# Moving one batch's query transposes behind sixteen score matmuls, and one re-lay one unit later, in an attention and gated feed-forward kernel

## The chip, the core and the metric

The kernel runs on one core of a Trainium2 chip. The core has five engines with a queue of instructions each: TensorE (PE in the profile; its weight loads are listed apart as PEld), VectorE (DVE), ScalarE (ACT), GpSimd (POOL) and SyncE (SP). They run side by side and wait for each other through semaphores. Matmul results land in a small accumulator memory, PSUM, of eight banks; everything else lives in SBUF. Transfers are carried out by 16 DMA engines. The metric is the device time of one execution in microseconds, as the median of several runs; less is better.

## The reference

Two stages follow one another. The first is attention with a sigmoid in the place of the softmax, for 8 batches, 12 heads, 448 positions and a head width of 64:

```python
scores = scale * np.matmul(q, k.transpose(0, 1, 3, 2)) - np.log(S)
attn = 1.0 / (1.0 + np.exp(-scores))
return np.matmul(attn, v).astype(np.float32)
```

Its output, seen as x with 8 · 448 = 3584 rows of 12 · 64 = 768 columns, goes through a gated feed-forward layer of width 1536:

```python
gate = np.maximum(x @ w_gate, 0.0)
val = x @ w_val
return (gate * val @ w_out).astype(np.float32)
```

Inputs and outputs are 32-bit floats; the kernel multiplies in 16 bits.

## The kernel before

**Tiling.** Heads are taken in three groups g of four. The 448 positions of a batch are seven chunks c of 64. Queries and keys have to lie transposed (head width on the partitions) before the scores can be formed; the transposed form of one group is a tile `qkT` with 14 blocks, seven for the keys and seven for the queries. The scores of one key chunk against all queries are a score unit: matmuls of 64x64 tiles at L259, four of them running side by side in the four quarters of TensorE's array, then a sigmoid on ACT (L187) into a tile `PT`. Seven such units give what the product with the values needs (`pv`, L277, again 64x64 tiles). DVE scales its result out of PSUM into `xT` (L184), which is the input of the feed-forward layer. A feed-forward unit (`gv`, L342) forms one 128-column block of gate and value: six full-array 128x128 matmuls `g_ps`, six `v_ps`, then a relu on ACT (L354) or DVE (L356) and a product on DVE (L363) into `hT`. From batch 1's end on, feed-forward products are formed with fewer multiplications from sums and differences of blocks (Strassen's scheme, L409, L738); DVE forms those sums at L400 and L597, and `T` from the weight `wo`.

**Order.** Nothing reorders instructions: `tc.manual_schedule()` leaves each engine's order as the program writes it, and waits are set from the data. PSUM banks go round in a ring: four banks in the first stage, eight later.

**Batch 0**, the first 29 us, has its own order. The queries are split in two halves, of 4 and 3 chunks (`QCUT` = 4), so that there are six slots: slots 0 to 2 are the groups with the first half of the queries, slots 3 to 5 the groups with the second. A slot has four score units `slot.unit(u)`: the first three hold two key chunks (8 matmuls each in slots 3 to 5, of 64x192), the last one chunk (4 matmuls). The scores of a unit go to one of two two-bank PSUM buffers (`pairp`, `bufs=2`), which alternate. So a unit cannot start before the sigmoid of the unit two before it has read that buffer. What TensorE does between the units is written in a table `after`, keyed by slot and unit; each entry runs right behind the unit named. In the parts that matter here it holds the `pv` of an earlier slot, `second_queries()` (the PE transposes, L204, of the second half of the queries of groups 1 and 2: 3 chunks x 2 heads x 2 groups = 12 matmuls against the identity, each 64 columns of the array wide, and two DVE copies L211 into `qkT`), and `ffn_mix(1)`, which takes one feed-forward unit off a queue (its first use takes a unit of 256 columns of batch 0).

**Batch 1** runs bursts of score units, each followed by `ffn_mix` with a number of feed-forward units (`mix`). Its `hooks` name what happens between the units of a burst: an entry `(n, job)` runs when n units of the mix are left. `steps` are DVE instructions that form weight sums, handed out between the units by the counts in `given`. When n units are left, the hooks come first, then the steps, then the unit.

**Re-lays.** From batch 2 on the transposes are left to the DMA: `dma_transposes(b, g)` has DVE copy the four heads' keys and queries (L242, two copies) into a tile `rel` (two buffers), and SP issues one transposing DMA from `rel` into `qkT` (L246). The last burst of batch 1 (burst 5, a mix of four units) has two hooks: `late_loads` with four units left, and the re-lay of batch 2's group 2 with two left.

**Loads.** POOL's queue issues the loads, converting to 16 bits, in program order. `late_loads` first makes POOL wait for the transposing DMA of batch 2's group 1 (`hold`, L887, a tiny copy), then loads v of batch 2 (L115, L117), k and q of batch 3 (L111; these overwrite batch 2's k and q and so wait for the copies L242 of the re-lay), and the weight `wo` in two parts (L164).

**Around the end.** Each `y` unit of the output projection goes to the result by SP's queue (L382), from 104 us on.

Of the kernel before, what the change touches and what calls it, by code (L numbers as in the profile page):

```python
# [18 lines left out]
def kernel(  # L19
# [170 lines left out]
    def qkT_of(b, g):  # L190
        if (b, g) not in qkT_tiles:
            qkT_tiles[(b, g)] = qkTp.tile([P, TW, P], FP16, tag="qkT", name="qkT")
        return qkT_tiles[(b, g)]

    def pe_transposes(b, g, ti, c0=0, c1=NCH):
        transposed(b, g, ti, c0, c1)()
# [21 lines left out]
    def quarter_transposes(b, g):  # L218
        qkT = qkT_of(b, g)
        trt = [bank16("trt") for _ in range(2)]  # L220
        for i in [*range(NCH, TW), *range(NCH)]:
            t16 = in_tiles[b][i // NCH]
            c = i % NCH
            for h in range(2):
                for r in range(2):
                    rows = slice(64 * r, 64 * r + 64)
                    nc.tensor.transpose(  # L227
                        trt[r][64 * h : 64 * h + 64, 64 * i : 64 * i + 64],
                        t16[rows, 2 * g + h, c * D : (c + 1) * D],
                        ident[rows, rows],  # L230
                    )
        for r in range(2):
            nc.vector.tensor_copy(
                qkT[:, :, 64 * r : 64 * r + 64],
                trt[r][:, 0 : TW * 64].rearrange("p (i x) -> p i x", i=TW),
            )

    def dma_transposes(b, g):
        k16, q16, _ = in_tiles[b]
        rel = relp.tile([P, TW, P], FP16, tag="rel", name="rel")  # L240
        for ti, t16 in enumerate((k16, q16)):
            nc.vector.tensor_copy(  # L242
                rel[:, ti * NCH : (ti + 1) * NCH, :].rearrange("p c (h d) -> p h c d", h=2),
                t16[:, 2 * g : 2 * g + 2, :].rearrange("p h (c d) -> p h c d", c=NCH),
            )
        nc.sync.dma_start_transpose(  # L246
            qkT_of(b, g)[:], rel[:].rearrange("p c x -> p (c x)")
        )
# [331 lines left out]
    def early_sum_steps(j, f):  # L580
        views = []
        for i in range(3 * j, 3 * j + 3):
            t = early.tile([P, 2, 512], FP16, tag=f"PT{i}", name="S")
            flat = t[:].rearrange("p a y -> p (a y)")[:, 0 : HD * 2 * P]
            views.append(flat.rearrange("p (x y) -> p x y", y=2 * P))
        yield lambda: gate_sums(f, f + 2)
        yield from unit_sum_steps(("s", f), f, views)
# [206 lines left out]
    def ffn_mix(count, hooks=(), steps=(), given=()):  # L794
        hooks = list(hooks)
        for left in range(count, -1, -1):
            while hooks and hooks[0][0] >= left:
                hooks.pop(0)[1]()
            for step in itertools.islice(steps, given[count - left] if steps else 0):
                step()  # L800
            if left:
                gv_queue.popleft()()
# [16 lines left out]
    slots = [FirstSlot(half * NG + g, g, half) for half in range(2) for g in range(NG)]  # L819
    push_first(0, range(0, 2), False)  # L820
    gv_queue.append(lambda: gv_two(0, 0, 64 * HALVES[0][1], 2))
    def second_queries():
        for g in range(1, NG):
            pe_transposes(0, g, 1, QCUT, NCH)
# [8 lines left out]
        keys(0, 3)  # L833
        keys(3, NCH)

    def pv_then_queries():
        slots[2].pv()
        second_queries()

    def two_pv():  # L840
        slots[3].pv()
        slots[4].pv()
# [12 lines left out]
        (2, 1): lambda: pe_transposes(0, 0, 1, QCUT, NCH),  # L855
        (2, 2): slots[0].pv,
        (2, 3): slots[1].pv,
        (3, 0): pv_then_queries,
        (3, 2): lambda: ffn_mix(1),
        (4, 0): lambda: ffn_mix(1),  # L860
        (4, 2): lambda: ffn_mix(1),
        (5, 0): two_pv,
# [86 lines left out]
    for b in range(1, B):  # L949
# [12 lines left out]
        if b == 1:  # L962
            mix = (4, 3, 3, 3, 3, 4)
            hooks = {
                1: [(3, lambda: quarter_transposes(1, 1))],
                4: [(2, lambda: dma_transposes(2, 0)), (0, lambda: dma_transposes(2, 1))],
                5: [(4, late_loads), (2, lambda: dma_transposes(2, 2))],
            }
            steps = itertools.chain.from_iterable(early_sum_steps(j, 2 * j) for j in range(4))
            given = ((0, 0, 1, 0, 2), (0, 1, 1, 1), (0, 1, 1, 1), (0, 1, 1, 0), (2, 0, 0, 0), (0, 1, 1, 1, 0))  # L970
        else:
            mix = (0,) * count
# [111 lines left out]
```

## Time and profile before

| | |
|---|---|
| median of 3 runs | 387.45 us (387.33 to 387.62) |
| profiled execution | 387.08 us |
| its span | 385.3 us |
| busy: PE / PEld | 379.8 us (99%) / 223.0 us |
| busy: DVE / ACT / POOL | 304.7 us (79%) / 227.2 us (59%) / 51.2 us (13%) |
| chain that ended last | PE 97%, ACT 2% |
| granted TensorE clock | 0.999 of full speed |
| DMA | 43.81 MB, mean 114 GB/s |

The span is the time from the first to the last recorded instruction; the profiled execution's own time, 387.08 us, is the span and 1.8 us around it. A row of the timeline has the start in us, the time for which the row's instructions run, the engine, the line, the operation, the tile written and the tile read, the shapes, the number of instructions merged into the row, and in brackets the idle time ahead of it and what ended it. Since matmuls are pipelined, the time from one row's start to the next row's start on PE is what a block costs, not the busy time beside it. A row of the windows has, for each stretch, its length, the busy time and the number of instructions of PE, PEld, DVE, ACT and POOL, the granted clock, the DMA share and the GB/s.

### The profile page before, as it was taken

Reading aid. Unit: us, or ns where it says so; the run is one execution under the profiler, and the core shown is the slowest. Engines: PE = TensorE matmul, PEld = TensorE weight load, DVE = VectorE, ACT = ScalarE, POOL = GpSimd, SP = SyncE. Lnnn points to the kernel's source line nnn. Section 1 sums busy time; section 2 is a strip of 40 time slices with the busy share of each in tenths; the row PEclk is TensorE's granted clock in tenths of the full one; section 3 lists DMA queues with packets and bytes.
Section 4 is the critical chain, followed back from the end, with each engine's and each line's share of the span. In section 5 each row is a group of like instructions: output and inputs, shape, how many; then the busy total and the mean of one; then the engine's idle time right before and its main releaser. Section 6 shows DMA issues by size and latency. Waiting matters only on the chain.

```text
span 385.3 us, 9098 instructions
## 1 busy us (share of the span) xinstructions
PE 379.8 (99%) x3626; PEld 223.0 (58%) x3626; DVE 304.7 (79%) x611; ACT 227.2 (59%) x480; POOL 51.2 (13%) x77
## 2 busy tenths in 40 slices
PE   8999999999999999999999999999999999999996
PEld 6678876885555545555555554545555555555664
DVE  3455668769868999999868789999978788999663
ACT  5967887558777645555777764545577344333322
POOL 9643305003300003000302300000000000000000
PEclk9999999999999999999999999999999999999999
DMA  9999999996998303952499994222012220000335
GB/s 174 198 199 204 204 200 142 207 204 109 169 209 196 83 0 43 171 100 49 70 242 146 204 213 80 48 49 48 2 40 71 72 68 2 0 2 0 77 89 164
DMA packets 67595, 43.81 MB, mean 114 GB/s; under 512 B 35680, under 2 KB 64224, under 8 KB 67552
## 3 DMA queue, kind: packets, MB, share of 16 engines
q0 software_dynamic: 28992, 23.24, 41.0%
q1 hardware_dynamic: 37792, 19.34, 25.0%
q10 hardware_dynamic: 768, 0.66, 0.6%
q8 instruction: 28, 0.46, 0.5%
q14 instruction: 15, 0.12, 0.1%
HBM read 47.19 MB, written 11.01 MB: 151 GB/s over the span
## 4 chain that ended last, share of the span: by engine, by line
PE 97%; ACT 2%; DVE 0%; issue 0%; ACTq 0%
PE u L409 35%; PE g L409 16%; PE y L409 12%; PE qk_ps L259 10%; PE pv_ps L277 8%; PE g_ps L342 5%; PE v_ps L342 5%; PE u L738 2%; PE g L738 2%; ACT PT L187 2%; PE warm_ps L175 1%; PE trt L204 1%; PE trt L227 0%; DVE qkT L211 0%; DVE ysb L564 0%
## 5 line engine op out<-in xcount | busy, mean ns | idle before, releaser
L187 ACT ACTIVATE PT<-qk_ps 128x448 f16<-128x448 f32 (+3 forms) x318 | 151.1, 584 | 79.2 <-PE qk_ps L259 79.0
L409 PEld LDWEIGHTS <-S 128*128 128x128 f16 x576 | 56.4, 98 | 45.9
L648 DVE TENSOR_TENSOR gsb<-g,gsb 128x448 f32<-128x448 f32 x72 | 42.7, 624 | 7.8 <-PE g L409 7.5
L259 PE MATMUL qk_ps<-qkT 64*64 64x448 f16 (+2 forms) x756 | 47.3, 336 | 0.6 <-ACT PT L187 0.3
L409 PEld LDWEIGHTS <-hT 128*128 128x128 f16 x318 | 29.5, 98 | 24.0 <-issue 6.1
L277 PE MATMUL pv_ps<-PT,v 64*64 64x448 f16 (+2 forms) x756 | 36.4, 329 | 0.2 <-ACT PT L187 0.2
L488 DVE SCALAR_TENSOR_TENSOR ysb<-y,ysb 128x384 f32<-128x384 f32 x33 | 18.4, 556 | 20.7 <-PE y L409 14.1
L184 DVE TENSOR_SCALAR xT<-pv_ps 128x448 f16<-128x448 f32 (+2 forms) x53 | 27.8, 566 | 7.1 <-PE pv_ps L277 5.9
L409 PEld LDWEIGHTS <-wg 128*128 128x128 f16 x216 | 20.1, 98 | 21.8 <-issue 4.3
L409 PEld LDWEIGHTS <-wv 128*128 128x128 f16 x216 | 21.1, 98 | 19.7
L470 ACT ACTIVATE ysb<-u 128x384 f32<-128x384 f32 x28 | 13.8, 491 | 30.9 <-PE u L409 26.8
L409 PE MATMUL u<-wo,hT 128*128 128x384 f16 x156 | 29.8, 327 | 0.0
L259 PEld LDWEIGHTS <-qkT 64*64 64x64 f16 x756 | 17.7, 105 | 20.4 <-issue 14.3
L277 PEld LDWEIGHTS <-v 64*64 64x64 f16 x756 | 21.4, 107 | 11.1 <-issue 0.6
L111 POOL DMA_DIRECT2D k<-in_k_dram x15 | 11.5, 770 | 93.8 <-DVE rel L242 88.1
L409 PE MATMUL u<-xT,wg 128*128 128x448 f16 x108 | 23.5, 354 | 0.0
L409 PE MATMUL g<-xT,wg 128*128 128x448 f16 x108 | 23.4, 352 | 0.0
L409 PE MATMUL u<-X,wv 128*128 128x448 f16 x108 | 23.4, 352 | 0.0
L409 PE MATMUL g<-xT,S 128*128 128x448 f16 x108 | 23.4, 352 | 0.0
L409 PE MATMUL g<-X,S 128*128 128x448 f16 x108 | 23.4, 352 | 0.0
L409 PE MATMUL u<-X,S 128*128 128x448 f16 x108 | 23.4, 352 | 0.0
L409 PE MATMUL u<-xT,wv 128*128 128x448 f16 x108 | 23.4, 352 | 0.0
(103 smaller groups left out, 563.7 us busy)
## 6 DMA issues: line engine op xcount, KB each, us to landing
out_dram<-ysb SPq DMA_DIRECT2D x53, 192.0 KB, 3.6
v<-in_v_dram POOLq DMA_DIRECT2D x8, 336.0 KB, 11.0
v<-in_v_dram POOLq DMA_DIRECT2D x16, 168.0 KB, 10.3
wo<-in_moe_w_out_dram POOLq DMA_DIRECT2D x2, 1152.0 KB, 19.8
k<-in_k_dram POOLq DMA_DIRECT2D x10, 224.0 KB, 11.8
k<-in_k_dram POOLq DMA_DIRECT2D x3, 672.0 KB, 12.0
q<-in_q_dram POOLq DMA_DIRECT2D x3, 672.0 KB, 14.6
q<-in_q_dram POOLq DMA_DIRECT2D x8, 224.0 KB, 12.2
```

What stands on the lines that cost most here:

```text
L111: nc.gpsimd.dma_start(t16[:, xs, cs], rows_of(src, b)[:, xs, cs])
L175: nc.tensor.matmul(ps[:, 0:n], zeros[:, 0:P], zeros[:, 0:n], start=True, stop=True)
L184: nc.vector.tensor_scalar(out=xT, in0=src, scalar1=XSCALE, scalar2=None, op0=AOP.mult)
L187: nc.scalar.activation(PT_ap, ps_ap, AF.Sigmoid, bias=sig_bias, scale=qk_scale)
L259: nc.tensor.matmul(out_of(hh)[o : o + 64, :], qkT[rows, c, cols], qkT[rows, NCH + c0 : NCH + c1, cols], start=True, stop=True, tile_positi ...
L277: nc.tensor.matmul(ps[hh][64 * r : 64 * r + 64, 0:qn], v16[rows, 2 * g + hh, c * D : (c + 1) * D], pieces[c][rows, hh, :], start=(c == 0), ...
L342: nc.tensor.matmul(ps[:, 0:qn], (wg, wv)[i][:, dc, f * P : (f + 1) * P], xT_tiles[b][:, dc, q0 : q0 + qn], start=(dc == 0), stop=(dc == ND ...
L409: nc.tensor.matmul(ps[:, 0:n], A[:, k_, :], W[:, k_, :], start=(first and k_ == 0), stop=(k_ == kn - 1), skip_group_check=True,)
L470: nc.scalar.activation(o, ps[:, 0:HM], AF.Copy, scale=OUT_SCALE)
L488: nc.vector.scalar_tensor_tensor(out=o, in0=ps[:, 0:HM], scalar=OUT_SCALE, in1=o, op0=AOP.mult, op1=AOP.add)
L648: nc.vector.tensor_tensor(out=gs[u][i][:], in0=ps[u][:, 0:S], in1=gs[u][i][:], op=AOP.add)
L738: nc.tensor.matmul(ps[j // 2][:, j % 2 * SQ : (j % 2 + 1) * SQ], sets[j][i][:, k_, :], W[:, k_, :], start=(first and j % 2 == 0 and k_ == ...
```

## The change

There are two edits. In batch 0's table, the twelve query transposes of `second_queries()` stood behind the `pv` of slot 2, after unit (3, 0). Now the `pv` of slot 2 stands there alone, units (3, 1) and (3, 2) follow it directly (sixteen score matmuls), and the transposes come behind unit (3, 2), in front of the feed-forward unit that was there already. In batch 1's last burst, the re-lay of batch 2's group 2 runs when one unit of the mix is left, not two. So on DVE its two copies change places with one weight sum (L597) and the product `hT` of the third feed-forward unit. The order on ACT, POOL and SP stays as it was; no instruction is added or taken away.

```diff
-    def pv_then_queries():
-        slots[2].pv()
+    def queries_then_unit():
         second_queries()
+        ffn_mix(1)
...
-        (3, 0): pv_then_queries,
-        (3, 2): lambda: ffn_mix(1),
+        (3, 0): slots[2].pv,
+        (3, 2): queries_then_unit,
...
-                5: [(4, late_loads), (2, lambda: dma_transposes(2, 2))],
+                5: [(4, late_loads), (1, lambda: dma_transposes(2, 2))],
```

## The prediction

> **What bounds the kernel now.** I read the page first, then TensorE's timeline around 17 us (the first edit) with ACT's rows beside it, then DVE, SP and POOL around 60 us (the second edit), and last the later readers of what those move.
>
> ```profile
> PE 379.8 (99%) x3626; PEld 223.0 (58%) x3626; DVE 304.7 (79%) x611; ACT 227.2 (59%) x480; POOL 51.2 (13%) x77
> PE 97%; ACT 2%; DVE 0%; issue 0%; ACTq 0%
> ```
>
> PE is busy 99% of the span and carries 97% of the chain, so an edit counts by what it does to PE's starts. Here is PE's timeline at the first edit, start to start:
>
> ```profile
> 15.62 0.96 PE L277 MATMUL pv_ps<-PT,v 64*64 64x256 f16 x28
> 16.38 0.36 PE L259 MATMUL qk_ps<-qkT 64*64 64x192 f16 x8
> 16.55 0.96 PE L277 MATMUL pv_ps<-PT,v 64*64 64x256 f16 x28
> 17.44 0.53 PE L204 MATMUL trt<-ident,q 128*64 128x128 f16 x12
> 17.89 0.52 PE L259 MATMUL qk_ps<-qkT 64*64 64x192 f16 x16
> 18.35 0.83 PE L342 MATMUL g_ps<-xT,wg 128*128 128x256 f16 x6
> ...
> 19.77 0.52 PE L259 MATMUL qk_ps<-qkT 64*64 64x192 f16 x12
> 20.22 0.83 PE L342 MATMUL g_ps<-xT,wg 128*128 128x256 f16 x6
> ```
>
> The same 28-matmul value product costs 0.76 us when scores follow (15.62 to 16.38) and 0.89 us when transposes follow (16.55 to 17.44). The scores are of the same 64*64 form as the product, the transposes are 128*64: a change of form costs about 0.13 us. Now ACT around it, each row from a narrow window:
>
> ```profile
> 16.86 0.81 ACT L187 ACTIVATE PT<-qk_ps 128x768 f16<-128x768 f32 x1
> 18.36 1.51 ACT L187 ACTIVATE PT<-qk_ps 128x768 f16<-128x768 f32 x2 [0.70 <-PE qk_ps L259]
> ```
>
> The first row is the sigmoid of unit (3, 0), which ends at 17.67; the second holds those of (3, 1) and (3, 2). ACT idles 0.70 us between them since the scores of (3, 1) come late. DVE at the second edit:
>
> ```profile
> 58.66 0.41 DVE L363 TENSOR_TENSOR hT<-gate_sb,v_ps 128x256 f16<-128x256 f32 x1
> 58.99 0.39 DVE L242 COPY rel<-k 128x896 f16<-128x896 f16 x1
> 59.29 0.39 DVE L242 COPY rel<-q 128x896 f16<-128x896 f16 x1
> 59.59 0.55 DVE L597 TENSOR_TENSOR S<-S,wg 128x768 f16<-128x768 f16 x1
> 60.06 0.35 DVE L363 TENSOR_TENSOR hT<-gate_sb,v_ps 128x192 f16<-128x192 f32 x1
> ...
> 60.80 0.35 DVE L363 TENSOR_TENSOR hT<-gate_sb,v_ps 128x192 f16<-128x192 f32 x1
> 62.36 0.62 DVE L184 TENSOR_SCALAR xT<-pv_ps 128x448 f16<-128x448 f32 x1 [1.22 <-PE pv_ps L277]
> ```
>
> DVE then has 1.22 us to spare. PE and the DMA later on:
>
> ```profile
> 60.00:65.00 5.00, 5.00 (x63) 2.56 (x60) 3.71 (x10) 4.37 (x10) 3.90 (x7) 1.00 0.79 126
> 80.00:85.00 5.00, 5.00 (x55) 5.00 (x54) 3.94 (x9) 3.37 (x8) 0.00 (x0) 1.00 1.16 211
> 105.00:110.00 5.00, 5.00 (x62) 2.84 (x59) 4.26 (x9) 4.45 (x10) 0.00 (x0) 1.00 1.40 143
> ```
>
> PE is busy throughout; the last column shows loads at 211 GB/s alone and 143 GB/s where a transposing DMA runs among them.
>
> **The first edit, step by step.** The new order on PE is value product, (3, 1), (3, 2), transposes, feed-forward unit.
> 1. Value product with scores behind it: 0.76, so (3, 1) starts at 16.55 + 0.76 = 17.31, not 17.89.
> 2. Eight scores take 0.17 (16.38 to 16.55), so PE reaches (3, 2) at 17.48. But its PSUM buffer is that of (3, 0), whose sigmoid ends at 17.67. PE resumes 0.05 after a sigmoid: at 28.85 a value product goes on, released by ACT, and the three sigmoids ahead of it end at 26.69 + 2.11 = 28.80. So (3, 2) starts at 17.72: a new wait of 0.24. Before, 17.67 had passed when PE got there. Behind it on PE stand the transposes and the feed-forward unit.
> 3. Sixteen scores with a change of form behind them take 0.46 (17.89 to 18.35). Less 0.19 for the first eight (0.17 and 0.02 for the slower start of that block after a change of form) this leaves 0.27 to 0.29, and the transposes start at 18.00.
> 4. The twelve transposes took 0.45 with scores behind them. With a 128*128 matmul behind them no warm row shows the price. Below: eight transposes followed by eight more take 0.25 (8.14 to 8.39) and followed by scores 0.32 (8.39 to 8.71), so without a change of form 0.45 less 0.07 to 0.09, about 0.36. Above: at 5.25 eight took 0.54 ahead of a 128*128 matmul, but the eight ahead of those took 0.42 against 0.25 at 8.14, so 0.17 of it is a slower array; 0.37 remains, 0.05 over 0.32, hence 0.50. I take 0.45, because the form changes here too. The unit starts at 18.45, bounds 18.36 to 18.50, against 18.35: +0.10 (+0.01 to +0.15).
> 5. A wait goes. Unit (4, 0) shares a buffer with (3, 2), whose sigmoid ended at 18.36 + 1.51 = 19.87, while PE was there at about 19.85. Twelve scores took 0.45 (19.77 to 20.22); sixteen with no such wait take 0.46 (17.89 to 18.35), four cost 0.08, so twelve should take 0.38. The sigmoids of (3, 1) and (3, 2) now come about 0.6 and 0.2 us sooner, hence -0.07.
>
> Sum: +0.03 us, bounds -0.06 to +0.08. The Trainium skill's page TensorEngine Tiling (Array Packing), section Key Properties, says that changing the tiling mode drains TensorE; by it three changes become two and the edit gains about one drain, -0.13 by the rows above. The rows agree that a change costs that; the rule leaves out the wait of step 2.
>
> Off the path: the two copies L211 (0.61) shift from 18.21 to about 18.4, end near 19.05, before DVE's next instruction at 19.22, and their reader (4, 0) comes at 19.85. `xT`, ready at 18.30, is in time for the unit. ACT keeps its order and waits for scores later too (0.28 at 20.15), so its lead is not passed on. No DMA, SP or POOL instruction moves here.
>
> **The second edit.** The third `hT` comes after its `v_ps` (58.85 + 0.66 = 59.51), at about 59.6 and not 60.06; the copies run at about 59.9 to 60.6, not 58.99 to 59.68; the last `hT` at about 60.98, not 60.80. Its bank is next written by the `g_ps` at 62.64, and DVE's 1.22 us of slack takes up the 0.18. A gain from the earlier third `hT` is excluded: PE waits for no bank here. SP issues the transposing DMA about 0.9 late (59.75 to 60.65); SP's next entry is at 81.78, so nothing queues behind it. POOL issues the load of k that waits for the copies at 63.28, 2.7 us after their new end; its hold waits for another group's DMA and opens at 60.80 as before. The DMA landed in 4.0 us, now 64.7. Its buffer `rel` is next written by DVE at 81.64, and its scores come after 87.7. If it took 17.4 us, as the one issued at 95.28 did among loads, it would land at 78.1, still in time. What it takes from the loads: `wo`'s second part landed at 65.8 + 22.1 = 87.9 and is first read at 93.15 (5.2 us to spare); q of batch 3 landed at 64.13 + 11.8 = 75.9 and is read at 81.33 (5.4). Full traffic of the transposing DMA is some 2 us, so at most 2 us of it moves into the loads. Cost 0 as long as the delay is under 5.2 us.
>
> Total +0.03 us: 387.08 becomes 387.11 in the profiled execution, which lies 0.37 under the median of the runs, so the median goes from 387.45 to 387.48, say 387.5. 0.2%, or 0.77 us, is about what a measurement of this kernel can tell from no change.
>
> **Rivals.**
> - The drain is saved and nothing takes its place: if (3, 2) is not held, step 2's 0.24 goes and the sum is -0.21: 387.25. For it speaks the 0.13 of the change of form; against it the buffers that alternate and the sigmoid's end at 17.67. It needs a sigmoid that ends before 17.43. This would still be no measurable change.
> - ACT's lead of 0.6 us is carried on to the end of batch 0. The PE waits on ACT that the views show are 0.3 us in the list of waits and 0.16 at 28.85, so with the rival above at most -0.7: 386.8; 0.2% is passed only if more such waits are hidden in blocks that the views show as busy. Against it: ACT waits for PE's scores, 79.0 us in the list, not the reverse.
> - Slower, by the loads. The transposing DMA no longer ends before the loads begin to move (about 63.6) and runs among them. At 143 against 211 GB/s over a landing of 17.4 us, the loads lose 17.4 x 0.32 = 5.6 us; `wo` would then come 0.4 late: 387.9. Held back over all 23 us of loads they lose 23 x (211/143 - 1) = 11 us, 5.8 beyond the margin: 393. It decides from 5.2 us of delay. Against it: at 95.28 the transposing DMA was issued 2 us behind the first loads, here it is issued 0.6 us ahead of them (61.28). The Trainium skill's page DMA: Bandwidth & Descriptors, section Queues, rings and completion order, says that a DMA engine takes turns between its queues packet by packet, which speaks for this rival. The rows above agree at 105 to 110 us, not at 80 to 85, though a transposing DMA was issued at 81.78.
>
> **How the numbers follow.** Forecast as summed (387.5): 0.58. Drain saved (387.25): 0.21. ACT's lead to the end: 0.06, of which 0.03 passes 0.2%. Loads: 0.07, of which 0.06 passes 0.2%. Something that no row shows: 0.08, of which 0.03 faster and 0.05 slower by over 0.2%. Faster by over 0.2%: 0.06; within: 0.83; slower: 0.11. The range 386.9 to 388.0 takes in the bounds of the first edit (387.2 to 387.55), the spread of the runs (0.17 up, 0.12 down) and the mild ends of the second and third rival.
>
> **What would show it.** Right: (3, 1) at 17.31, a stop of about 0.24 ahead of (3, 2) ended by ACT, transposes at 18.00, `g_ps` at 18.4 to 18.5, twelve scores in 0.38, and every later PE row shifted by under 0.1. The copies L242 at 59.9, the transposing DMA at 60.65, `wo` landed before 93. Wrong: `g_ps` before 18.25; a PE wait on DVE at L342 near 62.6; `T` from `wo` later than 93.2, or `rel` later than 81.7.

## The result, and the profile after

The changed kernel's median is 387.49 us (386.57 to 395.56, 22 executions), that of the kernel before, run beside it, 387.12 us (386.70 to 387.78, 22 executions). The ratio is 1.0023 with a 95% interval of 1.0012 to 1.0034: slower by 0.1 to 0.3%. The ratios leave out executions over 1.5% above the fastest of their kernel, here three, at 393.4 to 395.6 and a granted clock of 0.991 (below, in e2, one, at 392.71); what they lost besides the wait told below is not shown. The median hides the form of the loss: the two medians differ by 0.1% only, the means (387.97 without those three, 387.13 before) by 0.2%. Twelve executions lie between 386.57 and 387.49, where the kernel before lies; ten lie above 388, where it never was. So most executions lose nothing and some lose one to several microseconds.

The profiled execution, 390.15 us with a span of 388.4, is one of those that lose. From its page: the engines, the chain, and the group of the value products (count, then busy time, mean ns, and the idle time ahead with what ended most of it).

```profile
PE 379.9 (98%) x3626; PEld 222.7 (57%) x3626; DVE 305.1 (79%) x611; ACT 227.2 (59%) x480; POOL 52.0 (13%) x77
...
PE 89%; DMA 6%; ACT 3%; DVE 1%; POOL 1%; issue 0%; SPq 0%; POOLq 0%; ACTq 0%
...
L277 PE MATMUL pv_ps<-PT,v 64*64 64x448 f16 (+2 forms) x756 | 36.8, 329 | 3.0 <-DMA v<-in_v_dram 2.8
```

PE's work is the same to 0.1 us, but 6% of the chain is now DMA, and a value product waits 2.8 us for a load of v. The first edit, on PE's timeline of the same execution:

```profile
16.38 0.96 PE L277 MATMUL pv_ps<-PT,v 64*64 64x256 f16 x28
17.14 0.77 PE L259 MATMUL qk_ps<-qkT 64*64 64x192 f16 x16
17.84 0.53 PE L204 MATMUL trt<-ident,q 128*64 128x128 f16 x12
18.29 0.83 PE L342 MATMUL g_ps<-xT,wg 128*128 128x256 f16 x6
...
19.71 0.44 PE L259 MATMUL qk_ps<-qkT 64*64 64x192 f16 x12
20.08 0.83 PE L342 MATMUL g_ps<-xT,wg 128*128 128x256 f16 x6
```

This execution ran 0.17 us ahead from its first microseconds. From the value product's start, `g_ps` comes after 1.91 us (1.80 before), the next unit's `g_ps` after 3.70 (3.67 before): the first edit costs 0.03 us here. The second edit, on DVE:

```profile
58.55 0.41 DVE L363 TENSOR_TENSOR hT<-gate_sb,v_ps 128x256 f16<-128x256 f32 x1
58.88 0.55 DVE L597 TENSOR_TENSOR S<-S,wg 128x768 f16<-128x768 f16 x1
59.51 0.35 DVE L363 TENSOR_TENSOR hT<-gate_sb,v_ps 128x192 f16<-128x192 f32 x1
59.78 0.39 DVE L242 COPY rel<-k 128x896 f16<-128x896 f16 x1
60.08 0.39 DVE L242 COPY rel<-q 128x896 f16<-128x896 f16 x1
```

PE keeps its distance to the kernel before up to 105 us (0.11 ahead) and is 3.06 us behind at the first `u` after the stop (110.14 against 107.08). The chain of waits leads there (start, length, what):

```profile
86.19 7.38 DMA qkT<-rel
...
93.69 0.74 POOL gate L887
94.43 0.60 POOL v L115
...
95.11 0.62 POOL v L117
95.73 12.55 DMA v<-in_v_dram
...
108.32 1.51 PE pv_ps L277 x25
```

It reads as follows. A transposing DMA of batch 3 (group 1) is issued at 86.19 and lands at 93.57. The hold ahead of batch 3's v, a second hold with the same purpose as the one at 60.80, opens on it. The three pieces of v are issued at 94.37, 95.11 and 95.73; the last takes 12.5 us, and the value product that began at 105.16 stops until 108.32. The same steps before, POOL's rows and then SP's row of the next transposing DMA:

```profile
92.56 0.18 POOL L887 COPY gate<-qkT 1x2 f16<-1x2 f16 x1 [25.95 <-DMA qkT<-rel]
93.01 0.75 POOL L115 DMA_DIRECT2D v<-in_v_dram  x1 [0.27 <-PE qk_ps L259]
93.75 1.25 POOL L117 DMA_DIRECT2D v<-in_v_dram  x2
```

```profile
95.28 6.54 SPq L246 DMA_TRANSPOSE qkT<-rel  x1
```

There v's last piece was issued at 94.37 and landed 7.2 us later, at 101.6; its reader came at 105.27. That is 3.6 us to spare, and no list of waits shows it. The last piece's row, before and after (its size, then the us from issue to landing):

```profile
v<-in_v_dram POOLq DMA_DIRECT2D x1, 168.0 KB, 7.2
v<-in_v_dram POOLq DMA_DIRECT2D x1, 168.0 KB, 12.5
```

Two things changed: v is let off 1.36 us later, and its last piece takes 5.3 us longer.

The first has its cause in the second edit. The moved transposing DMA is issued at 60.54, not 59.75, and lands after 6.8 us, not 4.0, at 67.3, among the loads that begin at 61. `wo`'s second part lands after 23.5 us, not 22.1. The transposing DMAs behind those loads shift too: the one of group 0 keeps SP for 4.34 us and not 3.35, so that of group 1 is issued a microsecond later, and the hold opens at 93.69 instead of 92.56. The hold's tiny copy then takes 0.74 us instead of 0.18 (last section). The second, the longer landing, is what the experiments are about.

### The profile page after: what moved, and what is told of

The parts are those of the page before. It is cut to its first block, busy times and chain, and to the rows that moved or that the text cites. A ratio compares the mean times of both kernels' runs of the same rounds, so it can differ in the third digit from the quotient of the medians.

```text
span 388.4 us, 9098 instructions
## 1 busy us (share of the span) xinstructions
PE 379.9 (98%) x3626; PEld 222.7 (57%) x3626; DVE 305.1 (79%) x611; ACT 227.2 (59%) x480; POOL 52.0 (13%) x77
## 4 chain that ended last, share of the span: by engine, by line
PE 89%; DMA 6%; ACT 3%; DVE 1%; POOL 1%; issue 0%; SPq 0%; POOLq 0%; ACTq 0%
PE u L409 33%; PE g L409 16%; PE y L409 11%; PE qk_ps L259 8%; PE pv_ps L277 7%; PE g_ps L342 4%; PE v_ps L342 4%; DMA v<-in_v_dram 3%; ACT PT L187 3%; PE u L738 2%; DMA qkT<-rel 2%; PE g L738 2%; DMA ysb<-in_k_dram 1%; PE trt L204 0%; PE trt L227 0%
## 5 line engine op out<-in xcount | busy, mean ns | idle before, releaser
L111 POOL DMA_DIRECT2D k<-in_k_dram x15 | 11.5, 767 | 93.3 <-DVE rel L242 88.1
L409 PE MATMUL u<-xT,wg 128*128 128x448 f16 x108 | 23.5, 354 | 0.0
```

What stands on the lines that cost most here:

```text
L111: nc.gpsimd.dma_start(t16[:, xs, cs], rows_of(src, b)[:, xs, cs])
L409: nc.tensor.matmul(ps[:, 0:n], A[:, k_, :], W[:, k_, :], start=(first and k_ == 0), stop=(k_ == kn - 1), skip_group_check=True,)
```

## The experiments

All comparisons are against the kernel before, run in the same sitting. Theory A, the load chain just told; theory B, the first edit. First each edit alone.

**e1, the first edit alone.** It is the change without this line:

```diff
-                5: [(4, late_loads), (2, lambda: dma_transposes(2, 2))],
+                5: [(4, late_loads), (1, lambda: dma_transposes(2, 2))],
```

> The first edit alone (the query transposes behind sixteen scores); the re-lay stays where it was. Theory A, the load chain: the late re-lay alone pushes batch 3's v into the transposing DMA of its group 2, so this kernel lacks the cause. It expects the median within 0.2 us of before (ratio 1.000 +- 0.001), no execution above 388, PE's wait on the load of v at about 105 us absent, and g_ps in the first edit about 0.1 later and the scores behind it about 0.03 later than before, measured from the value product. Theory B, the first edit is the cause (the PE order, or the earlier sigmoids, shift what follows): ratio 1.002 or more and single executions at 389 to 395.

Measured: median 387.07 against 387.05, ratio 1.0002 (0.9993 to 1.0011), highest 388.01, just over the limit that I had named. PE never waits for v. PE's timeline:

```profile
16.56 0.96 PE L277 MATMUL pv_ps<-PT,v 64*64 64x256 f16 x28
17.33 0.77 PE L259 MATMUL qk_ps<-qkT 64*64 64x192 f16 x16
18.02 0.53 PE L204 MATMUL trt<-ident,q 128*64 128x128 f16 x12
18.48 0.83 PE L342 MATMUL g_ps<-xT,wg 128*128 128x256 f16 x6
...
19.90 0.44 PE L259 MATMUL qk_ps<-qkT 64*64 64x192 f16 x12
20.27 0.83 PE L342 MATMUL g_ps<-xT,wg 128*128 128x256 f16 x6
```

`g_ps` comes 1.92 us after the value product (1.80 before); twelve scores take 0.37 (0.45 before). The end of the stretch is 3.71 us off against 3.67. The first edit is worth nothing that can be measured, and theory B falls.

**e2, the second edit alone.** Only the line shown above is changed.

> The second edit alone (the re-lay one unit later). Theory A: as the changed kernel, a spread from 386.8 to 395 us with a third or more of the executions above 388; the transposing DMA issued at about 60.7 lands 6 to 7 us later, not 4.0; the hold before batch 3's v opens at 93 to 94, not 92.6; v's last piece takes over 10 us to land in the executions that stop, and PE waits for it at 105. Theory B: as before, no execution above 388.

Measured: median 387.22, ratio 1.0025 (1.0000 to 1.0049). Eight of twelve executions lie between 386.8 and 387.5, four between 389.7 and 392.7. The profiled one (389.71) has the stop. SP's row, POOL's rows, and PE's row after it:

```profile
61.32 1.52 SPq L246 DMA_TRANSPOSE qkT<-rel  x1
```

```profile
94.15 1.06 POOL L887 COPY gate<-qkT 1x2 f16<-1x2 f16 x1 [27.11 <-DMA qkT<-rel]
95.16 0.74 POOL L115 DMA_DIRECT2D v<-in_v_dram  x1
```

```profile
107.85 1.33 PE L277 MATMUL pv_ps<-PT,v 64*64 64x448 f16 x24 [1.55 <-DMA v<-in_v_dram]
```

(This execution ran 0.7 us late from 20 us on, after a wait for weights that has nothing to do with the edit.) The moved transposing DMA landed after 7.1 us and v's last piece after 11.3. The second edit alone brings the stop and a loss of the same size, so it carries the loss, as far as an interval from 1.0000 to 1.0049 can tell.

**e3, the next transposing DMA out of v's way.** The changed kernel, with the re-lay of batch 3's group 2 behind the unit.

```diff
-                ahead += [lambda: weight_sums(1), lambda: dma_transposes(3, 2)]
-                jobs += first_sums[2:]
+                ahead += [lambda: weight_sums(1)]
+                jobs += [*first_sums[2:], lambda: dma_transposes(3, 2)]
```

> The changed kernel, with the re-lay of batch 3's group 2 (two copies and the transposing DMA, at about 94 us) put behind that stretch's feed-forward unit, so the transposing DMA is issued about 2.5 us later (near 98 instead of 95.4) and v of batch 3 has most of its packets through. Theory A with contention (v is slow because it shares the DMA engines with that transposing DMA): v's last piece lands in 5 to 8 us, no PE wait at 105, no execution above 388, median about 387.0. Theory A with lateness alone (v is late because the hold opens late, whatever else moves): the hold still opens at 93 to 94 and the stops stay as in the changed kernel.

Measured: median 387.18, ratio 1.0009 (1.0000 to 1.0018), highest 388.25. v is let off at 94.47, as late as in the changed kernel, the transposing DMA at 97.70; v's last piece lands in 5.2 us and PE does not wait for it. So in the profile v was slow because of that neighbour, not because the hold opened late. Two of eleven executions still lie just above 388 (388.02 and 388.25); what they lose is not shown.

**e4, v behind `wo`.** The changed kernel, with batch 3's v issued in batch 2's first stretch, right behind `wo`.

```diff
-                jobs += [lambda: hold(3, 1), lambda: load_v(3)]
+                jobs += [lambda: hold(3, 1)]
...
-                if b not in (2, 5):
+                if b != 5:
                     jobs.append(lambda: load_v(b + 1))
```

> The changed kernel, with batch 3's v issued right behind wo (about 76 us) and not behind the hold. Theory A: v lands at about 91 to 93, 12 us before its use, so the PE wait at 105 goes; 672 KB more in front of the transposing DMAs of batch 3's groups 0 and 1 delay those by about 3 us, to 96, with their first use behind that. Median 387.0, no execution above 388. If another reader of the late loads is the one that stops PE (k and q of batch 4, or the transposing DMA itself), single executions stay at 389 to 395.

Measured: median 387.97, ratio 1.0023 (1.0012 to 1.0033), 386.97 to 388.81. The wait for v is gone, and another took its place, as the weight loads' row shows:

```profile
95.42 0.14 PEld L259 LDWEIGHTS <-qkT 64*64 64x64 f16 x8 [0.53 <-DMA qkT<-rel]
```

The transposing DMA of batch 3's group 0, issued at 82.11, had the extra 672 KB in front of it and landed after 13.3 us, at 95.4, where its first scores were due. My expectation that its first use lies behind 96 was wrong. The readers of these loads that were looked at have 3.6 to 5.4 us of slack, no more.

**Later, by how much?** If a late v is the cause, a later v should be worse. Two kernels hold v longer in the kernel before, with neither edit (seven and fifteen hold copies), one moves the re-lay one unit further, and one holds the loads at 61 us until the moved re-lay has landed.

```diff
-                jobs += [lambda: hold(3, 1), lambda: load_v(3)]
+                jobs += [lambda: hold(3, 1)] * 7 + [lambda: load_v(3)]
```

> The kernel before, untouched in both edits, with the tiny hold copy on POOL ahead of batch 3's v done seven times and not once, which lets that v off about 1.5 to 2.5 us later (94.5 to 95.5, not 93.0). The re-lay at 59 us and the loads behind it are as before. If the late start of that load is all that it takes (it then meets the transposing DMA issued at 95.3): v's last piece lands in 9 to 13 us, PE waits for v near 105 in some executions, the times spread from 387 to 391. If the overlap of the earlier re-lay with the loads at 61 to 85 us does something more (a slower DMA from then on), this kernel stays as before, under 388.

> The same with fifteen hold copies: v is let off 3 to 4 us later than before (96 to 97), wholly behind the transposing DMA's issue. Late start theory: v lands at 108 or later in nearly every execution, PE waits 3 us or more at about 105, median 390 or more, few executions under 388. Otherwise as before.

```diff
-                5: [(4, late_loads), (1, lambda: dma_transposes(2, 2))],
+                5: [(4, late_loads), (0, lambda: dma_transposes(2, 2))],
```

> The changed kernel, with the re-lay of batch 2's group 2 one unit later still (no unit of the mix left): its transposing DMA is issued at about 61.5 and then lies wholly among the loads. Load chain theory: the transposing DMA lands 7 us or more later, the loads end 1.5 to 2.5 us later than before (against 1.1 in the changed kernel), v is let off at 94.5 or later, more executions stop and for longer: median 388 or more. If the size of the overlap does not matter: as the changed kernel, median 387.5.

```diff
-        hold(2, 1)
+        hold(2, 2)
...
-                5: [(4, late_loads), (1, lambda: dma_transposes(2, 2))],
+                5: [(1, lambda: dma_transposes(2, 2)), (0, late_loads)],
```

> The changed kernel, with the loads held until the transposing DMA of batch 2's group 2 has landed (the hold names group 2, and late_loads comes behind the re-lay). That DMA is then alone again and lands in about 4.0 us, at 64.7; the loads begin about 3.5 us later than before (65 against 61.3). If the overlap as such is what hurts, this is as before, under 388. If lateness hurts, whatever it comes from, wo lands at about 91.5, v is let off at 96 or later and PE stops for 3 us or more at 105: median 390 or more.

Measured against 386.94: e5 387.08, ratio 1.0001 (0.9993 to 1.0010); e6 386.97, 0.9999 (0.9990 to 1.0008); e7 386.95, 1.0007 (0.9996 to 1.0018), one execution at 389.08; e8 387.04, 1.0001 (0.9993 to 1.0010). Lateness alone has fallen: in e6 v was let off at 97.66, 4.6 us later than before, and nothing was lost. In e8 the loads began 3.3 us late and nothing was lost. In e7 the transposing DMA landed after 11.5 us, the hold opened at 95.47, and the loss nearly vanished. What these have in common is that v went off behind the transposing DMA of group 2, not ahead of it. The new theory, the coincidence, is that v is slow when it is issued about a microsecond ahead of that DMA. What lateness was expected to do in e6, e7 and e8, medians from 388 up, did not come.

**e9, e10, e11: the distance set by hand.** Three and four hold copies in the kernel before, five in the changed one; the edit is the one of e5 with another count.

> The kernel before with three hold copies ahead of batch 3's v: v is let off at about 93.4, some 1.8 us ahead of the transposing DMA issued at 95.2. Coincidence theory (the harm comes only where v's loads are issued from about 1.5 to 0 us ahead of that transposing DMA, so that both are half begun together): outside the window, v's last piece lands in 7 to 9 us, no wait at 105, under 388. Plain lateness has fallen with the long holds and expects nothing here.

> The kernel before with four hold copies; the fourth waits for DVE's long sum (93.2 to 94.5), so v is let off at about 94.6, some 0.6 us ahead of the transposing DMA, and less late than with seven copies (95.4), which did no harm. Coincidence theory: v's last piece lands in 9 to 13 us, PE waits for v at 105 in several executions, the times spread from 387 to 390, though neither edit of the change is in this kernel. If it takes the overlap of the earlier re-lay with the loads at 61 to 85 us: as before, under 388.

> The changed kernel, with five hold copies, so that v is let off later still, at about 95.6, 0.2 us behind the transposing DMA and not 1.0 us ahead of it. Coincidence theory: the later start cures it: v's last piece lands in about 7 us, no PE wait at 105, no execution above 388, median 387.0. If the harm of the second edit comes some other way, the spread to 390 and more stays.

Measured against 386.98: e9 387.06, ratio 1.0004 (0.9995 to 1.0013), highest 387.34; e10 387.16, 1.0007 (0.9994 to 1.0019), one of eleven executions at 389.41 where the theory expected several; e11 386.86, 0.9998 (0.9989 to 1.0006), highest 387.30. In e9 the third copy was held up too, so its distance was 0.7 and not 1.8 us. In e10 the profiled execution has no wait; v's last piece took 9.0 us and arrived at 104.9, just as PE came. e11 is the sharpest: the changed kernel, with v let off still later, loses nothing. Its POOL rows and SP's row:

```profile
93.39 2.04 POOL L887 COPY gate<-qkT 1x2 f16<-1x2 f16 x5 [26.93 <-DMA qkT<-rel]
95.48 0.75 POOL L115 DMA_DIRECT2D v<-in_v_dram  x1
```

```profile
94.99 1.53 SPq L246 DMA_TRANSPOSE qkT<-rel  x1
```

**e12, the coincidence alone.** The kernel before, with only the re-lay of group 2 pulled forward, so that v is not late at all but has the distance of the changed kernel.

```diff
-                ahead += [lambda: weight_sums(1), lambda: dma_transposes(3, 2)]
+                ahead += [lambda: dma_transposes(3, 2), lambda: weight_sums(1)]
```

> The kernel before, neither edit in it, with one change near 93 us: the re-lay of batch 3's group 2 stands in front of the weight sum that it followed, so its transposing DMA is issued at about 94.0, not 95.3, and batch 3's v, let off at 93.0 as before, is then 1.0 us ahead of it, the same distance as in the changed kernel, with v itself not late at all. Coincidence theory: v's last piece lands in 9 to 13 us, at 104 to 107, PE waits for v at 105 in a part of the executions, the times spread from 387 to 389 or more. If v's own lateness is needed too: v's last piece lands by 103, no execution above 388.

Measured: median 387.16 against 386.91, ratio 1.0011 (0.9995 to 1.0028), one of twelve executions at 390.56 and the next at 387.81. POOL, SP and PE:

```profile
92.87 0.17 POOL L887 COPY gate<-qkT 1x2 f16<-1x2 f16 x1 [26.18 <-DMA qkT<-rel]
93.32 0.75 POOL L115 DMA_DIRECT2D v<-in_v_dram  x1 [0.28 <-issue]
```

```profile
94.33 3.14 SPq L246 DMA_TRANSPOSE qkT<-rel  x1
```

```profile
105.52 1.70 PE L277 MATMUL pv_ps<-PT,v 64*64 64x448 f16 x28
```

v's last piece took 11.0 us and arrived at 105.7; the value product stretched to 1.70 us (1.49 before). So the distance makes v slow with neither edit in the kernel, but a v that is 1.05 us earlier than the changed kernel's mostly gets through: the interval takes in 1, and only the profile and the one execution at 390.56 speak of harm. All profiles but e4's, whose v goes elsewhere, side by side, ordered by distance, which is v's first issue less the transposing DMA's (the last piece's arrival is its issue and its time to landing):

| kernel | v issued | transposing DMA | distance | v's last piece lands in | arrives | PE waits |
|---|---|---|---|---|---|---|
| e3 | 94.47 | 97.70 | -3.2 | 5.2 | 101.0 | 0 |
| e1 | 92.71 | 95.28 | -2.6 | 6.6 | 100.7 | 0 |
| before | 93.01 | 95.28 | -2.3 | 7.2 | 101.6 | 0 |
| e12 | 93.32 | 94.33 | -1.0 | 11.0 | 105.7 | 0.3 |
| changed | 94.37 | 95.38 | -1.0 | 12.5 | 108.3 | 2.8 |
| e2 | 95.16 | 96.16 | -1.0 | 11.3 | 107.8 | 1.5 |
| e9 | 94.39 | 95.09 | -0.7 | 8.8 | 104.7 | 0 |
| e10 | 94.50 | 94.84 | -0.3 | 9.0 | 104.9 | 0 |
| e5 | 95.44 | 95.18 | +0.3 | 7.3 | 104.1 | 0 |
| e11 | 95.48 | 94.99 | +0.5 | 7.7 | 104.5 | 0 |
| e7 | 95.92 | 95.19 | +0.7 | 7.2 | 104.5 | 0 |
| e8 | 95.58 | 94.73 | +0.9 | 7.7 | 104.6 | 0 |
| e6 | 97.66 | 94.99 | +2.7 | 5.5 | 104.5 | 0 |

The landing time has its peak at a distance of -1.0 and falls to both sides, whichever edits are in the kernel. PE comes at 104.7 to 106, so only a piece that takes 11 us or more stops it in these profiles, and by how much depends on how late it was let off. The kernels below the middle of the table get through with less than 1.2 us to spare, against 3.6 before. Each row is one execution.

The three pieces of v, issued one by one, say more than the distance. In the three rows with a wait the transposing DMA is issued between v's second piece and its third (in the changed kernel at 95.38, between 95.11 and 95.73): the first two land in 4.8 to 5.9 us, and the third alone is slow. In e9 and e10 it is issued between the first and the second: the first lands in 5.3 to 5.4 us, the other two in 8.1 to 9.0. With all three behind it (e5, e7, e8, e11) they take 6.7 to 7.7. So slow are the pieces that come behind the transposing DMA when others of v went ahead of it, slowest where only the last does; "a microsecond ahead" is the distance at which that happens.

That the unprofiled executions differ by the same distance is an inference from the spread. Why the peak lies there is open: no view shows the order in which a DMA engine takes its packets. No kernel here beats the one before; e11 equals it.

## Why the prediction was wrong

The forecast was no measurable change, at 387.5. The comparison says slower, by 0.23% (0.12 to 0.34); I had given slower by over 0.2% a chance of 0.11. That the median falls on 387.5 is luck: the kernel before ran at 387.12 beside it, not at 387.45, and the median says nothing of the executions that stop.

- **The first edit was right in mechanism and size.** Each step, measured in e1 from the value product's start: scores at 0.77 (0.76 forecast), transposes at 1.46 (1.45), `g_ps` at 1.92 (1.90), twelve scores in 0.37 (0.38), the sum +0.04 (+0.03). The stop of about a quarter microsecond ahead of unit (3, 2) is there (sixteen scores take 0.69 and not 0.46), and the change of form that is saved (0.13) and the shorter twelve scores (0.08) nearly pay for it. The price for a change of form between transposes and a 128*128 matmul, which no warm row of before showed, is 18.48 - 18.02 = 0.46, the 0.45 taken and not the lower bound. This agrees with the Trainium skill's page TensorEngine Tiling (Array Packing), section Key Properties, which has the array drain at any change of tiling mode.
- **The second edit's own steps were right on DVE, PE and SP.** The third `hT` at 59.51 (59.6), the copies from 59.78 (59.9), the last `hT` at 60.85 (60.98), the transposing DMA at 60.54 (60.65), and no wait of PE near 62.6.
- **The step that failed is "Cost 0 as long as the delay is under 5.2 us".** It took the delay of the loads and held it against two readers, `wo` and batch 3's q. The delay was about right: `wo`'s second part landed at 89.0, 1.1 us later, within the 2 us allowed. The list of readers was too short, and "nothing queues behind it", said of SP, looked no further than the next entry's start. The loads end in front of the transposing DMAs of batch 3's groups 0 and 1; the second hold opens on those; v of batch 3 hangs on the hold, with 3.6 us to spare at its reader. And the margin was no constant either: moving v by 1.36 us put its last piece behind the next transposing DMA, and the landing took 5.3 us longer. A margin is only a margin while the transfer's own duration stays, and here it depends on what runs beside it.
- **"now 64.7"** for the moved transposing DMA's landing was a term too small: 67.3, after 6.8 us in place of 4.0.
- **The third rival** looked for the harm in the right kind of place, a transposing DMA among loads, and had the place, the reader and the threshold wrong: not `wo` from 5.2 us on, but v, for which 1.36 us were enough and 4.6 us (e6) harmless. Its price of 143 against 211 GB/s was misread too: the stretch from 105 to 110 holds 1.1 us (106.5 to 107.6) in which only 10 GB/s moved, so 143 is no rate of sharing. The row at 95.28 that it quoted, a transposing DMA that took 17.4 us among loads, was the very neighbour of the v that stops, and I used it only as a price for another one.
- The first two rivals did not occur. (3, 2) was held, and ACT's lead was not passed on: the wait of 0.16 at the end of batch 0 is still there (at 28.87 in e1).

## What to carry to other kernels

When a transfer is moved, follow the chain of transfers to its end: which loads it displaces, which transfers queue behind those, which hold opens on them, and what that hold lets off. For each, note the arrival against the reader's start, even where no wait is listed; a margin of 3.6 us with no entry in the list of waits was all that stood between this kernel and a stop. Two transfers that are released by different engines can meet or miss each other by a microsecond, so the harm can come and go between executions (an inference from the spread), and more delay can cure it. A median over a few executions tells little of such an edit; look at the spread.

## What the runs showed of the hardware that I had not expected

**The order of two starts, a microsecond apart, decides how long a load and a transposing DMA take.** Behind the transposing DMA (e5, e7, e8, e11), v's last piece lands in 7.2 to 7.7 us and the transposing DMA in 6.3 to 7.3. With v's first piece 1.0 us ahead (e12, e2, the changed kernel), both are slow: v's last piece 11.0 to 12.5 us and the transposing DMA 13.0 to 14.7. With v 2.3 us ahead, as before, v's last piece is through in 7.2 and the transposing DMA alone pays, with 17.4. The stretches of the changed kernel show busy DMA engines that move little (the last two columns are the DMA share and the GB/s), and in the last stretch PE's busy time of 0.52 us, behind the length of 2.00:

```profile
101.00:103.00 2.00, 2.00 (x21) 1.06 (x21) 0.86 (x3) 1.48 (x4) 0.63 (x1) 1.00 1.40 82
103.00:105.00 2.00, 2.00 (x20) 1.05 (x20) 1.55 (x4) 1.38 (x4) 0.00 (x0) 1.00 1.36 136
105.00:107.00 2.00, 0.52 (x11) 0.09 (x3) 1.53 (x3) 2.00 (x5) 0.00 (x0) 1.00 1.40 140
```

In the same stretches e5 moved 183, 180 and 204 GB/s. A slow stretch alone does no harm: e1 has 97 GB/s from 101 to 103 too, but there v had landed at 100.7. The Trainium skill's page DMA: Bandwidth & Descriptors, section Queues, rings and completion order, says that an engine goes round its queues one packet at a time. That a load and a transposing DMA slow each other here fits it, but no view shows the packets' order, and how much the order of two starts changes both is not to be had from it.

**A long sum on DVE holds up a tiny copy on POOL.** The hold's copy of two elements takes 0.17 to 0.18 us alone. In four of the profiles it met DVE's sums for `T` (1.35 us each) and ended with them: in the changed kernel at 94.43 with the sum ending at 94.39, in e1 at 92.77 (92.73), in e2 at 95.21 (95.17), in e3 at 94.52 (94.48). DVE's and POOL's rows of the changed kernel:

```profile
93.04 1.35 DVE L400 TENSOR_TENSOR T<-wo,T 128x2304 f16<-128x2304 f16 x1
```

```profile
93.69 0.74 POOL L887 COPY gate<-qkT 1x2 f16<-1x2 f16 x1 [27.39 <-DMA qkT<-rel]
```

So of the 1.36 us by which v went off late, 1.13 are the hold's opening (93.69 against 92.56) and 0.56 the copy's stay behind DVE's sum; 0.33 came back since no gap followed the copy. The Trainium skill's page SBUF — State Buffer, section Terms, says that VectorE and GpSimd contend for one pair of ports, which one of them has for a whole instruction while the other stands still; the four end times agree. POOL's issuing of loads, in the kernel before, ran beside such a sum (93.01 to 95.00 against 93.15 to 94.50) at its usual 0.63 to 0.75 us each. Nor was the slow piece slow in its issue: v's second and third took 1.25 us together in the changed kernel (95.11 to 96.36), as before (93.75 to 95.00).
